# Summing graph messages per node: plain f32 products with the message stationary, and a transposed aggregate

## The chip, the cores and the metric

The kernel runs on one core of a Trainium2 chip. The metric is device time in microseconds, the median of several runs. A core has five engines that run side by side, each with its own queue in program order: TensorE (PE; its weight loads are shown apart as PEld), VectorE (DVE), ScalarE (ACT), GpSimd (POOL) and SyncE (SP, which here only issues DMAs).

## What is computed

One layer of message passing on a graph: 12,500 nodes with 64 features, 800,000 edges with 16 features, a source and a destination node.

```python
N, deg, D, De = 12500, 64, 64, 16
E = N * deg

def reference(x, e_attr, src, dst, w_msg, w_upd):
    N, D = x.shape
    m_in = jnp.concatenate([x[src], x[dst], e_attr], axis=-1)
    msg = _silu(m_in @ w_msg)
    agg = _segment_sum(msg, dst, N)
    return _silu(jnp.concatenate([x, agg], axis=-1) @ w_upd)
```

All is f32. Edges come in no order, so the sum over the edges of a node needs a sort or a scatter.

## The kernel before

**Tables.** The product with `w_msg` is split: `x @ w_msg[0:64]` is computed once per node and kept in HBM as `A_d`, from where it is gathered by source; `x @ w_msg[64:128]` is kept in SBUF as `BW`, in 128 buckets of 98 nodes (`NBK`, `BK`), with the 16 rows for the edge features below each bucket's 98. So a tile of 128 edges of one bucket gets its message from one product: a matrix with a one-hot of the destination within the bucket and the 16 edge features (98 + 16 = 114 columns, `KQ`), times the bucket's 114 x 64 block of `BW`, plus the gathered rows of `A_d`.

**Sorting.** 6250 columns of 128 edges each go through steps of 8 columns (`M`). A step makes one-hots of the bucket (`onehot`, L392 and L393), running sums of them (`sums`, L399 to L406, bf16), ranks by matmuls (`count`, L419 to L422, and `ranks`, L427), spreads the edge records over slots (`expand`, L440) and moves them into bucket order by f32 matmuls (`move`, L460). A finished block is scattered to the store `st` in HBM by an indirect DMA on POOL (`scatter`, L483).

**Batches.** When buckets hold enough edges, a group of 64 tiles is formed on the core (`Group`): a work list says which bucket and which tile, in units of 1, 2 or 4 consecutive tiles (`u`; `QU` = 4 for most of the run: 656 of 818 batches). SP reads the list and loads the records into `rt`. A batch is 8 tiles (6 with units of 2). Its steps lie in four successive periods: `gather` (one indirect DMA of POOL per tile, L643) and `onehot` (L648) in the first; `transpose` of the one-hots (L657, copied by ACT at L660) and `product` (L666) in the second; `message` (DVE adds the gathered rows, L672; ACT takes the silu, L673) and `parts` in the third; `reduce` and `add` in the fourth.

**The sums before.** For units of 4, `parts` splits the f32 message into three bf16 parts by two subtractions on DVE (L681), and `reduce` multiplies the one-hot (stationary, 98 columns, read as bf16) with the three parts at once (moving, 192 columns, L692), summing over the unit's four tiles in PSUM. `add` folds the three parts (L705) and adds each unit's 98 x 64 block to the aggregate `ACC` at an offset read from the list (L707). For units of 1 and 2 the product is plain f32 with the one-hot stationary and the message moving (L694), two passes a product. The last 16 batches, one tile per bucket, add with one instruction (L699).

**Order.** It is written out by hand in `period`: each period issues, for the batches and steps at their several stages, gathers and the scatter on POOL, then the rest, engine by engine in this order. Gather tiles `g` have three buffers (`gp`) and are free again after `message`; PSUM tiles have one buffer each. `next_step` asks for the loads of edge indices (segments of `SEG` columns, in `sg`) and features (`ea`, `rec`, in `eap`) some steps ahead. After the last step come batches alone, and beside the last batches the updates: `Update.run` transposes two buckets of `ACC` at a time (L956), copies them (L958), multiplies with `wu` (L960), adds the stored `x @ w_upd[0:64]` (L962), and takes the silu.

Of the kernel before, what the change touches and what calls it, by code (L numbers as in the profile page):

```python
# [3 lines left out]
F32 = mybir.dt.float32  # L4
# [29 lines left out]
QU = 4  # L34

# [5 lines left out]
SEG = 15 * M  # L41
# [5 lines left out]
def mpnn_kernel(tc, x, e_attr, src, dst, w_msg, w_upd, out):  # L47
# [23 lines left out]
    with es:  # L71
# [17 lines left out]
        io_i = cp.tile([P, P], I32, name="io_i")  # L89
# [7 lines left out]
        ident = cp.tile([P, P], F32, name="ident")  # L97
# [13 lines left out]
        nc.vector.tensor_scalar(out=b64, in0=ipf, scalar1=float(D), scalar2=None, op0=OP.mult)  # L111

# [17 lines left out]
        wu = cp.tile([P, 2, D], F32, name="wu")  # L130
        wx = cp.tile([P, 2, D], F32, name="wx")
# [5 lines left out]
        sent = cp.tile([P, 32, R], F32, name="sent")  # L137
# [26 lines left out]
        class Nodes:  # L164
# [27 lines left out]
            def product(t, ps, w, c):  # L192
                for i in range(0, t.n, 2):
                    nc.tensor.matmul(ps[0:BK, i * c:(i + 2) * c], t.xt[:, i // 2 * BK:(i // 2 + 1) * BK], w.rearrange("p k c -> p (k c)"), start=True, stop=True)  # L194
                return ps[0:BK, 0:t.n * c].rearrange("p (i c) -> p i c", c=c)
# [28 lines left out]
        eap = pool("eap", 3)  # L224
# [92 lines left out]
        for w in (wab, wx, wu):  # L317
            nc.gpsimd.memset(w, 0.0)
# [12 lines left out]
        ACC = lp.tile([BK, NBK, D], F32, name="ACC")  # L331
        ACCf = ACC.rearrange("p b d -> p (b d)")
# [7 lines left out]
        zeros = [RT[i].rearrange("p a c -> p (a c)") for i in range(len(RT))] + [ACC[:, b:b + ZP, :].rearrange("p b d -> p (b d)") for b in range(0, NBK, ZP)]  # L340

        def later():
            z = zeros.pop(0)
            nc.scalar.activation(z, done0[0:z.shape[0], :].to_broadcast(z.shape), AF.Copy)
            if len(zeros) == 7:
                for k in range(P // 32):
                    nc.sync.dma_start(st_t[D0:D0 + DUM, k * 32 * R:(k + 1) * 32 * R], sent[0:DUM].rearrange("p a b -> p (a b)"))
            elif len(zeros) == 5:
                nc.sync.dma_start(BW[BK:KQ], w_msg[2 * D:2 * D + DE, None, :].to_broadcast([DE, NBK, D]))
            elif not zeros:  # L350
                for k in range(2):
                    nc.sync.dma_start(wx[k * D:(k + 1) * D, k, :], w_upd[0:D, :])
                    nc.sync.dma_start(wu[k * D:(k + 1) * D, k, :], w_upd[D:2 * D, :])
# [7 lines left out]
        rbp = pool("rbp", 6)  # L361
        qp = pool("qp", 4)
        qtp = pool("qtp", 2)
        gp = pool("gp", 3)
        mp = pool("mp", 2)
# [124 lines left out]
        class Group:  # L490
# [82 lines left out]
            def middle(g):  # L573
# [5 lines left out]
                elif g.k == 1:  # L579
# [3 lines left out]
                    nc.tensor.matmul(g.ps[0:1, gu:2 * gu], b64, mat[:, 0:gu], start=True, stop=True)  # L583

            def rows(g):
                gu = g.gu
                g.row, g.rb = wp.tile([1, GT], I32, name="row"), rbp.tile([1, GT], I32, name="rb")
# [124 lines left out]
        def period(step=None, batch=None, ptr_new=None):  # L712
# [44 lines left out]
            if a:  # L757
                a.parts()
# [410 lines left out]
```

## Time and profile before

| | |
|---|---|
| median of 3 runs | 11796.37 us (11699.31 to 11822.43) |
| span of the profiled execution, first to last instruction | 9112.0 us |
| POOL busy, and its 6322 gathers | 6777.5 us, 6201.1 us |
| DVE busy, and its 1312 subtractions of L681 | 8127.3 us, 904.8 us |
| PE busy, and its 5248 bf16 passes of L692 | 8088.1 us, 582.4 us |
| ACT busy | 5111.9 us |
| mean granted TensorE clock | 0.963 |

The span is that of the profiled execution; its time around the span is not given apart, and the median of the runs is 2684 us longer than the span. In the profile, a line of a group reads: source line, engine, operation, out<-in with shapes, count, then busy microseconds and mean nanoseconds of one, then the engine's idle time just before them and what ended it. A line of stretches has the stretch and its length, then busy time and instruction count of PE, PEld, DVE, ACT and POOL, the granted clock, the DMA share and GB/s. A line of waits reads: engine, tile and line that waited, what released it, microseconds in total, times, longest. A line of the timeline has start and length in microseconds.

### The profile page before, as it was taken

To read this page: it belongs to the slowest core of one execution; us is meant where nothing else is said; L and a number is where in the kernel's file an instruction comes from. 1 tells how busy PE (TensorE), PEld (TensorE's weight loads), DVE (VectorE), ACT (ScalarE), POOL (GpSimd) and SP (SyncE) were. 2 spreads that over 40 slices of the span, in tenths; PEclk is the share of its full clock that TensorE was granted. 3 is DMA by queue.
4 is the path that set the end of the run, shared out by engine and by line. 5 is a ranking of instruction groups with operands and counts; after the bars stand their busy time and mean duration, and the time that the engine had idled before them with its cause. 6 is when DMAs were issued, how large, how long until landed. Compare 5 with 4: busy or idle time off the path is not lost. (4 is left out here: it accounts for less than half of the span.)

```text
span 9112.0 us, 146201 instructions
## 1 busy us (share of the span) xinstructions
PE 8088.1 (89%) x43940; PEld 5887.5 (65%) x44702; DVE 8127.3 (89%) x17569; ACT 5111.9 (56%) x12617; POOL 6777.5 (74%) x6910
## 2 busy tenths in 40 slices
PE   8999999888988889888888888899888889888677
PEld 5777776666666666666666666666666666666676
DVE  8999999999999999999999999999999999998332
ACT  7666665555555555555555555555555555555222
POOL 1677777777777777777777777777777777777776
PEclk9999999999999999999999999999999999999566
DMA  3222221222221212211222212121212122121223
GB/s 75 55 60 60 62 63 51 52 53 53 53 53 51 56 49 54 56 50 50 54 53 53 55 51 53 52 56 49 55 50 55 51 54 54 51 55 47 58 47 50
DMA packets 650600, 492.45 MB, mean 54 GB/s; under 512 B 482888, under 2 KB 519304, under 8 KB 649800
## 3 DMA queue, kind: packets, MB, share of 16 engines
q0 software_dynamic: 238976, 349.72, 14.6%
q1 hardware_dynamic: 410503, 133.17, 6.7%
q8 instruction: 359, 5.88, 0.3%
q14 instruction: 442, 3.61, 0.1%
q10 hardware_dynamic: 320, 0.07, 0.0%
HBM read 330.05 MB, written 152.30 MB: 53 GB/s over the span
## 5 line engine op out<-in xcount | busy, mean ns | idle before, releaser
L643 POOL DMA_INDIRECT g<-A_d,sidx x6322 | 6201.1, 981 | 1947.5 <-issue 1473.6
L460 PE MATMUL pl<-X,hf 128*128 128x291 f32 (+5 forms) x12512 | 4093.8, 478 | 0.0
L460 PEld LDWEIGHTS pl<-X,hf 128*128 128x128 f32 x12512 | 2307.4, 191 | 1291.7 <-issue 937.8
L440 DVE TENSOR_TENSOR X<-cb,rec 128x442 f32<-128x442 f32 (+5 forms) x3128 | 2647.4, 909 | 27.1
L392 ACT ACTIVATE hf<-iof,shi 128x128 f32<-128x128 f32 x6256 | 1909.2, 389 | 1047.9 <-PE pl L460 1044.5
L666 PEld LDWEIGHTS pre<-w,qt 114*128 114x128 f32 x10496 | 1296.0, 195 | 317.3 <-issue 291.5
L666 PE MATMUL pre<-w,qt 114*128 114x64 f32 x10496 | 1268.9, 275 | 42.2 <-DVE msg L672 42.2
L673 ACT ACTIVATE msg<-msg 128x512 f32<-128x512 f32 (+1 forms) x818 | 501.9, 614 | 1276.8 <-DVE msg L672 1274.2
L672 DVE TENSOR_TENSOR msg<-pre,g 128x512 f32<-128x512 f32 (+1 forms) x818 | 546.1, 668 | 496.5 <-DMA g<-A_d,sidx 298.0
L660 ACT ACTIVATE qt<-tq 114x1024 f32<-114x1024 f32 (+1 forms) x818 | 801.8, 980 | 333.5 <-PE tq L657 330.1
L427 DVE TENSOR_REDUCE rank<-z 128x8 f32<-128x1024 f32 x782 | 949.2, 1214 | 29.9 <-PE z L422 28.1
L420 PE MATMUL z<-G,onesb 128*128 128x384 bf16 x1564 | 516.6, 330 | 486.4 <-DVE G L401 430.7
L681 DVE TENSOR_TENSOR msg<-msg 128x512 f32<-128x512 f32 x1312 | 904.8, 690 | 22.8
L393 ACT ACTIVATE hf<-hf,ones 128x1024 f32<-128x1024 f32 x782 | 899.0, 1150 | 25.4
L465 ACT ACTIVATE blk<-pl 128x512 f32<-128x512 f32 (+1 forms) x568 | 325.4, 573 | 1044.8 <-PE pl L460 911.1
L657 PE MATMUL tq<-ident,q 128*114 128x128 f32 x6322 | 887.9, 286 | 14.3 <-ACT nodes L190 13.0
L657 PEld LDWEIGHTS tq<-ident,q 128*114 128x114 f32 x6322 | 783.5, 142 | 140.8 <-ACT nodes L190 20.4
L692 PE MATMUL ag<-msg,q 128*98 128x192 bf16 x5248 | 582.4, 253 | 298.0 <-DVE rb L589 116.2
L483 POOL DMA_INDIRECT st<-blk,ptrs x567 | 568.7, 1003 | 322.4 <-issue 134.5
L648 DVE TENSOR_TENSOR q<-cb,lo 128x784 f32<-128x784 f32 (+1 forms) x818 | 768.5, 940 | 0.6
L692 PEld LDWEIGHTS <-q 128*98 128x98 bf16 x5248 | 497.7, 126 | 387.7 <-issue 327.9
L420 PEld LDWEIGHTS <-onesb 128*128 128x128 bf16 x1564 | 152.6, 98 | 424.3 <-DVE G L401 318.9
(145 smaller groups left out, 6694.0 us busy)
## 6 DMA issues: line engine op xcount, KB each, us to landing
g<-A_d,sidx POOLq DMA_INDIRECT x6322
ea<-in_e_attr SPq DMA_DIRECT2D x260, 192.0 KB
rt<-st SPq DMA_DIRECT2D x1312, 34.0 KB
st<-blk,ptrs POOLq DMA_INDIRECT x567
rt<-st SPq DMA_DIRECT2D x434, 8.5 KB
nodes<-in_x SPq DMA_DIRECT2D x62, 98.0 KB
rt<-st SPq DMA_DIRECT2D x320, 17.0 KB
A_d<-nodes SPq DMA_DIRECT2D x32, 98.0 KB
```

Source lines behind the costliest of these rows:

```text
L392: nc.scalar.activation(c.hf[:, k, :], iof, AF.Square, bias=c.hi[:, k:k + 1])
L393: nc.scalar.activation(c.hf, c.hf, AF.Relu, bias=ones, scale=-1.0)
L427: nc.vector.tensor_reduce(out=c.rank, in_=c.z, axis=AX.X, op=OP.max)
L440: nc.vector.tensor_tensor(out=c.x[:, k:k + 2, 2:2 + n * R].rearrange("p k (s c) -> p k s c", c=R), in0=hit[:, k:k + 2, 0:n, None].to_broad ...
L460: nc.tensor.matmul(pl[:, 0:w], c.hf[:, k, :], c.x[:, k, 0:w], start=(whole and n == c.size - 1), stop=ends)
L643: nc.gpsimd.indirect_dma_start(out=t.g[:, i, :], out_offset=None, in_=A_d, in_offset=bass.IndirectOffsetOnAxis(ap=t.grp.sidx[:, k:k + 1], ...
L648: nc.vector.tensor_tensor(out=t.q[:, 0:n, 0:BK], in0=ioB[:, None, 0:BK].to_broadcast([P, n, BK]), in1=t.grp.lo[:, i0:i0 + n, None].to_broa ...
L657: nc.tensor.transpose(t.tq[0:KQ, j * P:(j + 1) * P], t.q[:, j, :], ident)
L660: nc.scalar.activation(t.qt[:, 0:w], t.tq[0:KQ, 0:w], AF.Copy)
L666: nc.tensor.matmul(t.pre[:, i * D:(i + 1) * D], t.qt[:, i * P:(i + 1) * P], w, start=True, stop=True)
L681: nc.vector.tensor_tensor(out=t.msg[:, k + 1, :], in0=t.msg[:, k, :], in1=up[:, k, :, 1], op=OP.subtract)
L692: nc.tensor.matmul(t.ag[0:BK, u * w:(u + 1) * w].rearrange("p (k d) -> p k d", d=D), q[:, i, :], m[:, :, i * D:(i + 1) * D], start=(k == 0 ...
```

## The change

- `message` adds and takes the silu in place in the gather tile `g`; the tiles `msg` and `sum` and the step `parts` (L681) go. `gp` has four buffers in place of three.
- `reduce` is one plain f32 product per tile, whatever the unit: the message (128 edges x 64) is stationary, the one-hot (128 x 98) moving. The result is the transposed sum, 64 features on partitions by 98 nodes. Units go in pairs: one to PSUM partitions 0 to 63, the next to 64 to 127, with their tiles alternating.
- `ACC` becomes 128 partitions x 128 buckets x 98: the transposed aggregate, twice, one copy for each PSUM half. `add` adds a unit's 64 x 98 block from PSUM to the copy of its half; the fold L705 goes. The group's list `rb` gets a second row of offsets (steps of 98), made by one more small matmul.
- `Update.run` uses `ACC` as the stationary operand of one product per bucket, with `w_upd[64:128]` stored twice on 128 partitions (which adds the two copies): the transposes and their copy go.
- `ACC` takes more room, so other things shrink: segments of 72 columns, not 120 (`SEG`), two buffers of `ea` and `rec`, not three, five of `rb`, not six, a sentinel block of half the size written in eight DMAs, not four, `ident` and `wx` share room with other tiles, and the loads of `w_upd` come after the last step.

```diff
 QU = 4
+SR = 16
...
-SEG = 15 * M
+SEG = 9 * M
...
-        eap = pool("eap", 3)
+        eap = pool("eap", 2)
...
-        ACC = lp.tile([BK, NBK, D], F32, name="ACC")
-        ACCf = ACC.rearrange("p b d -> p (b d)")
+        ACC = lp.tile([2 * D, NBK, BK], F32, name="ACC")
+        ACCf = ACC.rearrange("p b k -> p (b k)")
...
-                for k in range(P // 32):
-                    nc.sync.dma_start(st_t[D0:D0 + DUM, k * 32 * R:(k + 1) * 32 * R], sent[0:DUM].rearrange("p a b -> p (a b)"))
+                for k in range(P // SR):
+                    nc.sync.dma_start(st_t[D0:D0 + DUM, k * SR * R:(k + 1) * SR * R], sent[0:DUM].rearrange("p a b -> p (a b)"))
...
-        rbp = pool("rbp", 6)
+        rbp = pool("rbp", 5)
...
-        gp = pool("gp", 3)
-        mp = pool("mp", 2)
+        gp = pool("gp", 4)
...
+                    nc.tensor.matmul(g.ps[0:1, 2 * gu:3 * gu], b98, mat[:, 0:gu], start=True, stop=True)
...
             def message(t):
-                w = t.n * D
-                t.msg = mp.tile([P, 3, BT * D], F32, name="msg")
-                u_ = t.msg[:, 2, :]
-                nc.vector.tensor_tensor(out=u_[:, 0:w], in0=t.pre[:, 0:w], in1=t.g.rearrange("p a b -> p (a b)")[:, 0:w], op=OP.add)
-                nc.scalar.activation(t.msg[:, 0, 0:w], u_[:, 0:w], AF.Silu)
-
-            def parts(t):
-
-                t.split = t.grp.u == QU
-                if t.split:
-                    up = t.msg.bitcast(BF16).rearrange("p k (f two) -> p k f two", two=2)
-                    for k in range(2):
-                        nc.vector.tensor_tensor(out=t.msg[:, k + 1, :], in0=t.msg[:, k, :], in1=up[:, k, :, 1], op=OP.subtract)
+                m = t.g[:, 0:t.n, :].rearrange("p a b -> p (a b)")
+                nc.vector.tensor_tensor(out=m, in0=t.pre[:, 0:t.n * D], in1=m, op=OP.add)
+                nc.scalar.activation(m, m, AF.Silu)
+
+            def half(t, j):
+
+                return slice(j % 2 * D, (j % 2 + 1) * D)
 
             def reduce(t):
                 t.ag = pag.tile([P, 512], F32, name="ag")
-                w = 3 * D
...
-                    if t.split:
-                        nc.tensor.matmul(t.ag[0:BK, u * w:(u + 1) * w].rearrange("p (k d) -> p k d", d=D), q[:, i, :], m[:, :, i * D:(i + 1) * D], start=(k == 0), stop=(k == t.grp.u - 1))
-                    else:
-                        nc.tensor.matmul(t.ag[0:BK, u * D:(u + 1) * D], t.q[:, i, 0:BK], t.msg[:, 0, i * D:(i + 1) * D], start=(k == 0), stop=(k == t.grp.u - 1))
+                u = t.grp.u
+                for j in range(0, t.n // u, 2):
+                    for k in range(u):
+                        for v in range(j, min(j + 2, t.n // u)):
+                            i = v * u + k
+                            nc.tensor.matmul(t.ag[t.half(v), v // 2 * BK:(v // 2 + 1) * BK], t.g[:, i, :], t.q[:, i, 0:BK], start=(k == 0), stop=(k == u - 1))
 
             def add(t):
...
-                s = t.ag[0:BK]
-                if t.split:
-                    nu = BT // QU
-                    s = mp.tile([BK, nu * D], F32, name="sum")
-                    nc.vector.tensor_reduce(out=s.rearrange("p (u d) -> p u d", d=D), in_=t.ag[0:BK, 0:nu * 3 * D].rearrange("p (u k d) -> p u d k", k=3, d=D), axis=AX.X, op=OP.add)
-                for u, a in enumerate(t.at(ACCf, ENG.DVE)):
-                    nc.vector.tensor_tensor(out=a, in0=s[:, u * D:(u + 1) * D], in1=a, op=OP.add)
+                for v, r in enumerate(regs(t.grp.rb[:, 1, :], t.i0 // t.grp.u, t.n // t.grp.u, ENG.DVE, (NBK - 1) * BK)):
+                    a = ACCf[t.half(v), ds(r, BK)]
+                    nc.vector.tensor_tensor(out=a, in0=t.ag[t.half(v), v // 2 * BK:(v // 2 + 1) * BK], in1=a, op=OP.add)
...
-            if a:
-                a.parts()
...
+        for k in range(2):
+            nc.sync.dma_start(wx[k * D:(k + 1) * D, k, :], w_upd[0:D, :])
+            nc.sync.dma_start(wu[k * D:(k + 1) * D, :], w_upd[D:2 * D, :])
...
-                for q in range(0, n, 2):
-                    nc.tensor.transpose(z[:, q // 2 * BK:(q // 2 + 1) * BK], ACC[:, b0 + q:b0 + q + 2, :].rearrange("p b d -> p (b d)"), ident[0:BK, 0:BK])
-                at = t.buf[:, BT * D:BT * D + BT // 2 * BK]
-                nc.scalar.activation(at[:, 0:(n + 1) // 2 * BK], z[:, 0:(n + 1) // 2 * BK], AF.Copy)
-                for q in range(0, n, 2):
-                    nc.tensor.matmul(z[0:BK, (BT + q) * D:(BT + q + 2) * D], at[:, q // 2 * BK:(q // 2 + 1) * BK], wu.rearrange("p k d -> p (k d)"), start=True, stop=True)
+                for q in range(n):
+                    nc.tensor.matmul(z[0:BK, q * D:(q + 1) * D], ACC[:, b0 + q, :], wu, start=True, stop=True)
```

64 lines of the change are left out of this document (32 added, 32 removed).

## The prediction

> **What bounds the kernel now.** I read the page first, then the busy time by stretch, then who waits on the gathering engine, then groups and timeline of one stretch. The page's chain of waits covers only the end of the run, where no edge is being sorted any more, so it says nothing of the rest.
>
> ```profile
> span 9112.0 us, 146201 instructions
> PE 8088.1 (89%) x43940; PEld 5887.5 (65%) x44702; DVE 8127.3 (89%) x17569; ACT 5111.9 (56%) x12617; POOL 6777.5 (74%) x6910
> ```
>
> By this line PE and DVE look like the bound and POOL does not. The next rows correct that. They are busy times of three stretches: batches of units of 2 tiles beside the sorting of edges (400 to 1150), units of 4 beside the sorting (1600 to 8350), and batches alone (8450 to 9060). Below them stands what POOL waited for in the middle stretch.
>
> ```profile
> 400.00:1150.00 750.00, 722.20 (x4374) 567.87 (x4458) 709.75 (x1893) 487.40 (x1217) 570.05 (x590) 1.00 0.24 61
> 1600.00:8350.00 6750.00, 6035.73 (x32382) 4254.91 (x32983) 6356.42 (x13123) 3881.29 (x9637) 5158.38 (x5220) 0.99 0.20 53
> 8450.00:9060.00 610.00, 445.12 (x2581) 422.30 (x2579) 212.99 (x560) 149.15 (x295) 457.15 (x481) 0.64 0.28 52
> ...
> POOL g L643 <- issue: 1103.0, 3617, 0.3
> POOL g L643 <- DMA g<-A_d,sidx: 260.4, 854, 0.3
> ```
>
> The longest wait in front of a POOL instruction is 0.3 us and the mean is 1103.0/3617 = 0.305 us: this is no wait for data but the step from one indirect DMA to the next, whatever releaser the view names. Counted in, POOL is full: 5158.38 + 5220 x 0.305 = 6750.5 of 6750 us, and 570.05 + 590 x 0.305 = 750.0 of 750. So the gathers and scatters on POOL set the pace in both stretches, to the microsecond, while PE stands at 96% in the first and 89% in the second, and DVE at 95% and 94%. An edit gains only what it takes off a POOL instruction, and loses only where another engine comes to need more than POOL's period.
>
> Groups of the middle stretch (busy time, mean in ns):
>
> ```profile
> L643 POOL DMA_INDIRECT g<-A_d,sidx x4819 | 4756.8, 987 | 1469.5 <-issue 1103.0 <-DMA g<-A_d,sidx 260.4 <-DVE q L648 44.5
> L483 POOL DMA_INDIRECT st<-blk,ptrs x401 | 401.9, 1002 | 122.3 <-issue 109.5 <-ACT blk L465 6.1 <-ACT rec L268 3.0
> L648 DVE TENSOR_TENSOR q<-cb,lo 128x784 f32<-128x784 f32 x603 | 583.2, 967 | 0.0
> L681 DVE TENSOR_TENSOR msg<-msg 128x512 f32<-128x512 f32 x1206 | 831.6, 690 | 21.0
> L705 DVE TENSOR_REDUCE sum<-ag 98x128 f32<-98x384 f32 x602 | 329.3, 547 | 0.0
> L707 DVE TENSOR_TENSOR ACC<-sum,ACC 98x64 f32 x1204 | 274.9, 228 | 43.7 <-DVE ACC L707 2.1 <-DVE sum L705 0.3 <-issue 0.3
> ```
>
> 603 one-hots are 603 batches, so a period lasts 6750/603 = 11.19 us, and 8 gathers of 0.987 + 0.305 with 0.665 scatters of 1.002 + 0.305 make 11.2.
>
> **What the change takes from POOL.** The gathers are as many as before. But they are not all equally long. POOL and DVE on the timeline from 3021 us on (start, length, engine):
>
> ```profile
> 3021.13 0.94 POOL L643 DMA_INDIRECT g<-A_d,sidx  x1 [0.30 <-issue]
> 3022.38 1.34 POOL L643 DMA_INDIRECT g<-A_d,sidx  x1 [0.30 <-issue]
> 3025.28 0.94 POOL L643 DMA_INDIRECT g<-A_d,sidx  x1 [0.30 <-issue]
> ...
> 3021.49 1.41 DVE L681 TENSOR_TENSOR msg<-msg 128x512 f32<-128x512 f32 x2
> 3022.82 0.97 DVE L648 TENSOR_TENSOR q<-cb,lo 128x784 f32<-128x784 f32 x1
> 3025.47 0.69 DVE L672 TENSOR_TENSOR msg<-pre,g 128x512 f32<-128x512 f32 x1 [0.55 <-DMA g<-A_d,sidx]
> ```
>
> A gather that starts while the two subtractions of L681 run (from 3021.49 for 1.41 us) takes 1.34 us in place of 0.94. One beside L672, also 512 elements wide, takes 0.94. L681 reads two operands from SBUF, L672 one from PSUM and one from SBUF. [...]
>
> The change drops L681 (the two subtractions that split a message in three bf16 parts) for every batch of units of 4. The means of the gather in the two stretches without L681 in their periods, the first with all the sorting on DVE, the second with DVE nearly idle (17 batches of it still have L681), and L681 in the second and in the whole run:
>
> ```profile
> L643 POOL DMA_INDIRECT g<-A_d,sidx x506 | 486.0, 961 | 154.3 <-issue 115.3 <-DMA g<-A_d,sidx 20.1 <-DVE G L401 5.5
> ...
> L643 POOL DMA_INDIRECT g<-A_d,sidx x476 | 453.1, 952 | 145.0 <-issue 131.0 <-DMA g<-A_d,sidx 12.5 <-DVE msg L672 0.6
> L681 DVE TENSOR_TENSOR msg<-msg 128x512 f32<-128x512 f32 x34 | 23.6, 693 | 0.6
> ...
> L681 DVE TENSOR_TENSOR msg<-msg 128x512 f32<-128x512 f32 x1312 | 904.8, 690 | 22.8
> ```
>
> So a gather gains between 0.987 - 0.961 = 0.026 and 0.987 - 0.952 = 0.035 us. L681 runs 1312 times in all, that is in 656 batches; 17 of them lie after the sorting, and 639 x 8 = 5112 gathers are touched: 133 to 179 us. I take the middle, 156 us, because the first row holds more bf16 sums per gather (6 gathers to a period, not 8) and the second none. The scatter gains nothing: 1.002 us here, and it is issued away from L681.
>
> **What it gives PE.** L692 (8 bf16 passes of 192 columns a batch) becomes 8 f32 products with the message (64 columns) stationary and the one-hot (98 columns) moving, two passes each. No row has that shape; its mirror (98 stationary, 64 moving, f32) is L694.
>
> ```profile
> 3009.66 1.03 PE L657 MATMUL tq<-ident,q 128*114 128x128 f32 x8
> 3010.58 0.89 PE L692 MATMUL ag<-msg,q 128*98 128x192 bf16 x8
> 3016.43 0.39 PE L456 MATMUL pl<-done,onesb 1*128 1x512 bf16 x1
> 3016.74 2.00 PE L460 MATMUL pl<-X,hf 128*128 128x223 f32 x8
> 3020.68 0.39 PE L419 MATMUL z<-hf,w 128*128 128x512 bf16 x1
> 3020.90 0.32 PE L420 MATMUL z<-G,onesb 128*128 128x384 bf16 x1
> ...
> 9024.72 1.52 PE L694 MATMUL ag<-msg,q 128*98 128x64 f32 x16
> ...
> L657 PE MATMUL tq<-ident,q 128*114 128x128 f32 x4824 | 642.2, 277 | 0.0
> L692 PE MATMUL ag<-msg,q 128*98 128x192 bf16 x4824 | 526.4, 251 | 278.8 <-DVE msg L681 107.2 <-DVE rb L589 106.6 <-DVE wl L550 61.6
> ```
>
> A burst of n passes lasts n - 1 spacings and the last pass's own 0.25 to 0.28 us. L657: (1.03 - 0.28)/7 = 0.107 us for 128 f32 columns, so 98 cost 0.082 and a load of 64, taken at the same rate, 0.054. L694: (1.52 - 0.25)/15 = 0.085, the longer of load and stream, not their sum of 0.136: the next load hides behind the stream. L692: (0.89 - 0.25)/7 = 0.091. New less old per batch: 16 x 0.085 - 8 x 0.091 = +0.63 us if loads hide as in L694 (taken: it is the same pair of sizes, swapped); 16 x 0.136 - 0.73 = +1.45 if they don't; 8 x 0.085 - 0.73 = -0.05 if the two PSUM halves run side by side.
>
> To this comes a change of the array's shape before and after the sums. L456, with one stationary row, is the nearest: 0.31 us to the next start, against 0.22 for the same 512 columns at L419. That is 0.09 a switch, 0.18 a batch. [...] I take +0.63 + 0.18 = +0.81 us.
>
> What PE has to spare in the middle stretch:
>
> ```profile
> PE z L420 <- DVE G L401: 394.3, 394, 2.5
> PE ag L692 <- DVE msg L681: 107.2, 232, 0.6
> PE ag L692 <- DVE rb L589: 106.6, 75, 2.4
> PE ag L692 <- DVE wl L550: 61.6, 62, 1.2
> ```
>
> 669.7/603 = 1.11 us a period, and before each of these 763 waits some 0.17 us of modelled tail (0.277 - 0.107) count as busy: 763/603 x 0.17 = 0.21, together 1.32. POOL's shorter period takes 8 x 0.026 = 0.21 of it. Left are 1.11 us for 0.81, so PE stays behind POOL, with 0.3 us or 3% idle. The stretch of units of 2 shows that 4% idle is enough. There L694 itself turns round, the sum of load and stream stays, and two switches (0.18) fit into the 4% of its period of 8.9 us (506/6 = 84 batches in 750 us).
>
> **The rest.** DVE loses 1.38 + 0.55 + 0.46 us a period and gets two additions of 98 columns from PSUM, by L707 about 0.23 to 0.27 each: some 1.9 us less, so it needs 6356.42/603 - 1.9 = 8.6 of 11 us. Three of the four waits above end with it. These additions read one operand from PSUM, like L672, so they take L681's place on POOL at nothing. The gather's tile is held until the sums are done, one period longer, and has a fourth buffer: POOL can still run as far ahead as now. Zeroing the wider ACC, halved segments, the smaller read-ahead and the end:
>
> ```profile
> L344 ACT ACTIVATE ACC<-done 98x2048 f32<-98x2048 f32 x4 | 7.7, 1924 | 0.0
> ...
> ACT rec L268 <- DMA ea<-in_e_attr: 10.3, 2, 7.5
> ...
> 9100.93 0.91 PE L956 MATMUL z<-ident,ACC 98*128 98x98 f32 x4 [0.79 <-DVE ACC L699]
> 9102.43 2.02 PE L960 MATMUL z<-wu,xu 128*98 128x128 f32 x8 [0.59 <-ACT xu L958]
> ```
>
> 98/64 of 7.7 us is 4 us more on ACT, before POOL is full. Two late loads in the whole run say that a buffer less is not missed: the queue of SP still issues them three periods ahead, and its eight half-size loads of sentinels, 34 more pairs of segment loads and the moved loads of the update weights meet no waiting reader; if one did, it is 7.5 us. The transpose and its copy leave the end (1.5 us from L956 to L960), 16 passes replace 8 there (about +0.8): -0.7 for each of the last three updates, -2 us.
>
> The sum is 9112 - 156 - 2 = 8954 us. The median of the runs, 11796.37 us, lies 2684 us above the span; nothing in the profile shows that part, and I keep it. 11796 - 158 = 11638, taken as 11640 us.
>
> **The rivals.** PE becomes the bound: the loads into half the array don't hide. Then PE needs 1.45 + 0.18 = 1.63 us more where 1.32 are free, 0.31 over POOL's present pace and 0.52 over the new one; without the tails in the slack it is 0.52 over the present. It is worse than before from +1.32 on, and gives nothing from +1.11 on. 639 x 0.31 to 0.52 = +200 to +330 us, 12000 to 12130; I put 12050. For it: the 3% are thin, and a step with the widest blocks has less. Against it: L694 hides its loads. Chance 0.22.
>
> The collisions only move: POOL falls onto the sums of L401 to L403, or the gather's extra is L648's, which starts under the same 1.34 us. Then the gathers stay near 0.98, 0 to 40 us are won, and the time is 11780. For it: the 1.34 us overlap both. Against it: 0.961 with L648 and the sums in every period. Chance 0.16.
>
> A stall in the loads or buffers, or a gain beyond 179 us by the halves in parallel, has 0.05. The forecast has 0.57; its own range is 11560 to 11710, from 179 + 2 and 133 with the runs' scatter of some 50 us about their median.
>
> **The numbers.** 1% is 118 us, about what a measurement can tell here; faster means under 11678. Of the forecast 0.46 lies there and 0.11 within 1%; of the moved collisions 0.02 and 0.13, with 0.01 slower; of the PE bound 0.01, 0.04 and 0.17; of the rest 0.02, 0.01 and 0.02. Sum: 0.51, 0.29, 0.20. The range goes from 11560 to 11860, over the second rival and the mild end of the first; its dear end is left out.
>
> **What would show it.** Right: the gather's mean near 0.955 us in the long stretch, no 1.34 us beside the message's path, POOL still full with 0.305 between, PE at 95 to 97%, 16 passes of the new sums in about 1.55 us, DVE near 78%. Wrong: waits of POOL above 0.3 us on PE's sums, or new passes 0.13 us apart (PE bound); gathers at 0.98 (collisions moved).

## The result, and the profile after

| | before | after | ratio, 95% interval |
|---|---|---|---|
| timed runs of the comparison, median | 11,809.4 us (4 runs) | 10,957.5 us (4 runs) | 0.9294 [0.9257, 0.9331] |
| span of the page | 9,112.0 us | 10,967.9 us | |

The change made the kernel 7% faster, where 1.3% was forecast. The two pages cannot be set against each other: the page of before shows an execution of 9,112 us, the page of after one of 10,968 us, and yet the change is faster. The plain reason is that this program, whichever of the two kernels, runs at two levels, and all runs timed together on one chip show one of them: on three chips the kernel before took 9,090 to 9,113 us, in all other runs (two chips more, and the timed runs above) 11,644 to 11,979. The page of before came from the quick kind, its timed runs and all of after's from the other; whether that page and those timed runs were of one chip is not on record. Each chip was met in one session only, so it is not shown that the level hangs on the chip and not on the session. Of what follows, each pair of numbers is from one kind.

The first lines of the page of after:

```profile
span 10967.9 us, 159910 instructions
PE 9041.8 (82%) x50244; PEld 6180.6 (56%) x50244; DVE 7181.8 (65%) x15722; ACT 5097.6 (46%) x12601; POOL 6586.9 (60%) x6908
```

Its busy times by stretch, from 1600 to 10200 us (units of 4 beside the sorting; the columns are length, busy time and count for PE, PEld, DVE, ACT and POOL, then granted clock, DMA share and GB/s):

```profile
1600.00:10200.00 8600.00, 7360.82 (x40968) 4910.85 (x40968) 5872.43 (x12354) 4157.95 (x10368) 5399.23 (x5649) 0.92 0.19 45
```

What its POOL waited for from 1600 to 8200 us (total, times, longest):

```profile
POOL g L641 <- issue: 1053.5, 3279, 5.3
POOL g L641 <- remote: 633.1, 284, 2.5
POOL g L641 <- ACT qt L658: 333.7, 121, 4.2
```

The prediction's arithmetic for POOL no longer closes: 5399.23 + 5649 x 0.305 = 7122 of 8600 us, 83%. POOL really waits here (2.2 us a time in the second row of waits), DVE is at 68%, PE at 86%, and no engine is full. The timeline of the same execution shows what they wait for (start, length, engine, line, and in brackets the idle time before):

```profile
5006.25 0.20 PE L581 MATMUL ps<-mat,b 128*1 128x16 f32 x2
5007.39 0.38 PE L419 MATMUL z<-G,onesb 128*128 128x512 bf16 x1
5007.60 1.04 PE L655 MATMUL tq<-ident,q 128*114 128x128 f32 x8
5008.69 0.94 POOL L641 DMA_INDIRECT g<-A_d,sidx  x1 [0.30 <-issue]
5009.94 0.94 POOL L641 DMA_INDIRECT g<-A_d,sidx  x1 [0.30 <-issue]
5012.45 0.17 DVE L586 SCALAR_TENSOR_TENSOR row<-ps,iof 1x16 int32<-1x16 f32 x1 [3.64 <-remote]
5012.64 1.02 ACT L658 ACTIVATE qt<-tq 114x1024 f32<-114x1024 f32 x1 [4.00 <-remote]
5012.64 1.20 DVE L424 TENSOR_REDUCE rank<-z 128x8 f32<-128x1024 f32 x1
5012.82 1.54 PE L682 MATMUL ag<-q,g 128*64 128x98 f32 x15 [4.18 <-remote]
```

tq is recorded as done at 5008.6; its reader, ACT, is free and starts 4 us later, at 5012.64. ps (small products that form the next group) is recorded as done at 5006.45; its reader, DVE, is free from 5008.8 on, starts at 5012.45, and comes to z, done at 5007.8, only after that. PE itself stands until 5012.8, apparently because its sums go into the PSUM buffer that ps holds until DVE has read it. "Remote" is the view's word where it finds no signal to name. On the quick kind the same hand-offs take nothing. I put the mean over some 270 to 550 hand-offs of each sort together (1800 to 7800 us), from the later of the recorded end of TensorE's work and of the reader's own instruction before, to the reader's start (pl holds the moved edge records, which ACT copies out):

| us | sums to DVE | z to DVE | tq to ACT | pl to ACT |
|---|---|---|---|---|
| before, quick kind (before_rep) | 0.00 | 0.00 | 0.01 | 0.03 |
| after, quick kind (after_rep) | 0.07 | 0.00 | 0.01 | 0.02 |
| after, other kind (after_timed) | 1.73 | 1.89 | 3.27 | 0.03 |
| before without L681 (before_noparts), other kind | 2.39 | 1.62 | 1.54 | 0.51 |

So on the other kind of chip the readers of the sums, of z and of tq start 1.5 to 3.3 us late on average in these two kernels (over 0.5 us late in 237 to 396 of some 450 cases in after_timed); the copy of pl does not in the changed kernel. With no engine full I take these hand-offs to set the time there. No run takes the lateness away, so this is inferred and not shown. I call those the late chips, the others the quick ones.

### The profile page after: what moved, and what is told of

The parts are those of the page before. It is cut to its first block, busy times and chain, and to the rows that moved or that the text cites. A ratio compares the mean times of both kernels' runs of the same rounds, so it can differ in the third digit from the quotient of the medians.

```text
span 10967.9 us, 159910 instructions
## 1 busy us (share of the span) xinstructions
PE 9041.8 (82%) x50244; PEld 6180.6 (56%) x50244; DVE 7181.8 (65%) x15722; ACT 5097.6 (46%) x12601; POOL 6586.9 (60%) x6908
## 5 line engine op out<-in xcount | busy, mean ns | idle before, releaser
L641 POOL DMA_INDIRECT g<-A_d,sidx x6322 | 5995.0, 948 | 3825.7 <-issue 1748.0
L457 PE MATMUL pl<-X,hf 128*128 128x291 f32 (+5 forms) x12512 | 4481.4, 504 | 297.3 <-issue 289.5
L457 PEld LDWEIGHTS pl<-X,hf 128*128 128x128 f32 x12512 | 2423.4, 201 | 1920.4 <-issue 1539.4
L693 DVE TENSOR_TENSOR ACC<-ag,ACC 64x98 f32 x1938 | 497.4, 257 | 1937.9 <-remote 1443.9
L682 PE MATMUL ag<-q,g 128*64 128x98 f32 x12644 | 893.7, 283 | 434.4 <-remote 273.9
L655 PE MATMUL tq<-ident,q 128*114 128x128 f32 x6322 | 1048.2, 320 | 68.7 <-ACT nodes L193 40.7
L655 PEld LDWEIGHTS tq<-ident,q 128*114 128x114 f32 x6322 | 928.0, 162 | 237.0 <-issue 101.1
L682 PEld LDWEIGHTS ag<-q,g 128*64 128x64 f32 x12644 | 704.6, 157 | 619.0 <-remote 281.5
L416 PE MATMUL z<-hf,w 128*128 128x512 bf16 x1564 | 650.9, 416 | 5.3 <-ACT hf L390 4.7
L668 DVE TENSOR_TENSOR g<-pre,g 128x512 f32<-128x512 f32 (+1 forms) x818 | 541.2, 662 | 100.3 <-issue 60.7
```

The lines of the kernel that those rows point to most:

```text
L457: nc.tensor.matmul(pl[:, 0:w], c.hf[:, k, :], c.x[:, k, 0:w], start=(whole and n == c.size - 1), stop=ends)
L641: nc.gpsimd.indirect_dma_start(out=t.g[:, i, :], out_offset=None, in_=A_d, in_offset=bass.IndirectOffsetOnAxis(ap=t.grp.sidx[:, k:k + 1], ...
L655: nc.tensor.transpose(t.tq[0:KQ, j * P:(j + 1) * P], t.q[:, j, :], ident)
L682: nc.tensor.matmul(t.ag[t.half(v), v // 2 * BK:(v // 2 + 1) * BK], t.g[:, i, :], t.q[:, i, 0:BK], start=(k == 0), stop=(k == u - 1))
```

## The experiments

**Both kernels again, with a profile each.** No edit.

> The kernel before, unchanged, for a trace of an execution whose span can be set against its time. The trace of before had a span of 9112 us while its runs took 11700 to 11833 us; the trace of the changed kernel has a span of 10968 us with a time of 10970, so only 2 us lie around a span. Theory 1 (two modes: the trace of before was a rare fast execution, the timed ones are slow inside the program): span within 10 us of the time, near 11.8 ms, and TensorE's semaphores come late, by 1 us and more after the recorded ends, as in the changed kernel (0.013 us in the trace of before). Theory 2 (2.7 ms lie outside the program of before alone): span near 9112 us beside a time near 11.8 ms, semaphores at 0.013 us.

> The changed kernel, unchanged. If it too has two modes (theory 1), a repeat may fall near 8950 us, the sum of the prediction, with POOL full (gaps of 0.305 us between its DMAs); if it is slow whenever it runs, 10955 to 10970 us again, with gaps on POOL of over 1 us on TensorE's late semaphores.

A quick chip: 9,102.8 and 8,926.5 us, ratio 0.981 (one run each; a second run of before took 9,098.1). That is 176 us gained, where 158 was worked out. Neither theory of before_rep came out as it was stated: the trace is a quick one beside a quick time. But its span, 9,101.0 us, lies 2 us below its time, so nothing like 2.7 ms stands outside of this program. Busy times by stretch, 1600 to 8200 us, of before_rep:

```profile
1600.00:8200.00 6600.00, 5884.99 (x31685) 4152.25 (x32276) 6219.89 (x12845) 3796.74 (x9430) 5043.63 (x5108) 1.00 0.23 53
```

and the group of its gathers there (count, busy time, mean in ns, idle time):

```profile
L643 POOL DMA_INDIRECT g<-A_d,sidx x4715 | 4651.2, 986 | 1436.9 <-issue 1167.8 <-DMA g<-A_d,sidx 172.8 <-DVE q L648 37.5
```

The same two views of after_rep:

```profile
1600.00:8200.00 6600.00, 6138.24 (x37457) 4272.14 (x38061) 5515.65 (x11438) 3884.47 (x9664) 5004.77 (x5235) 0.99 0.24 54
```

```profile
L641 POOL DMA_INDIRECT g<-A_d,sidx x4833 | 4603.1, 952 | 1472.8 <-issue 1186.3 <-DMA g<-A_d,sidx 172.2 <-PE ag L682 29.3
```

And the new sums on its timeline, right behind the transposes:

```profile
5022.29 1.03 PE L655 MATMUL tq<-ident,q 128*114 128x128 f32 x8
5023.26 0.90 PE L682 MATMUL ag<-q,g 128*64 128x98 f32 x16
```

POOL is full in both: 5043.63 + 5108 x 0.305 and 5004.77 + 5235 x 0.305 are 6601 of 6600 us. The gather went from 986 to 952 ns. 5112 gathers by 0.034 us are 174 us, nearly the whole gain.

**Is it the second operand in SBUF?** The changed kernel with the two subtractions back on DVE as idle work, into a scratch tile; once with both operands in SBUF (after_sub), once with the second in PSUM (after_psum). Room for the scratch comes from a smaller tile of sentinels, written in more pieces.

```diff
# after_sub
+            def parts(t):
+                if t.grp.u == QU:
+                    for k in range(2):
+                        scr = mp.tile([P, BT, D], BF16, name="scr")
+                        nc.vector.tensor_tensor(out=scr, in0=t.g, in1=t.g.bitcast(BF16).rearrange("p a (b two) -> p a b two", two=2)[:, :, :, 1], op=OP.subtract)
...
# after_psum
+                        nc.vector.tensor_tensor(out=scr, in0=t.g, in1=cb.rearrange("p (a b) -> p a b", b=D), op=OP.subtract)
```

They ran first on a late chip, beside the changed kernel, and later on a quick one.

> The changed kernel, unchanged, timed against the kernel before on one chip. Theory C (POOL sets the pace, L681 lengthened its gathers): 8926 against 9098 us, ratio 0.981, in every round. Rival (the 0.929 of the first comparison is the change itself): ratio 0.93 again. If some executions fall into the mode with late TensorE semaphores, both kernels are some 2000 us longer in it.

> The changed kernel with two subtractions of L681's kind put back at their old place, both operands in SBUF, results unused (bf16 scratch; sentinels in 32 smaller DMAs for room). Theory C: the gathers' mean goes from 0.952 back to about 0.985 us in the long stretch and the time rises by 0.033 x 5112 = 170 us, to about 9095. Rival D (it is DVE's load or the order of work that the change relieved, not the operands): a rise too, but the same one with a PSUM operand. Rival E (the gathers' length has nothing to do with it): 8926.

> The same two subtractions, of the same length, with the second operand from PSUM. Theory C: the gathers stay at 0.952 us and the time at 8926 (within 20). Rival D: as long as with two SBUF operands, about 9095.

> after_sub again: the changed kernel with the two subtractions of 8x64 per partition put back as idle work on DVE, both operands in SBUF. Where the changed kernel takes 8,926 us: the gathers go from 952 to about 977 ns as in after_sub, and 5,112 of them by 0.025 us make +128 us, so 9,020 to 9,080; if the subtractions cost nothing there, 8,920 to 8,960. Where it takes about 11,050: 11,050 to 11,150 as before.

> after_psum again: the same two subtractions with the second operand in PSUM. Where the changed kernel takes 8,926 us: DVE is as busy as in after_sub_b, but the gathers stay near 950 ns, so 8,920 to 8,960; if DVE's time and not the operands' place made the cost, the time of after_sub_b. Where it takes about 11,050: 11,050 to 11,180.

| | late chip | quick chip |
|---|---|---|
| before | 11,915.3 | 9,106.3 |
| after | 11,102.1, ratio 0.931 [0.9254, 0.9366] | not run beside them; 8,926.5 for after_rep |
| after_sub | 11,124.6, ratio 0.933 [0.9274, 0.9388] | 9,111.0, ratio 1.0006 [0.9997, 1.0016] |
| after_psum | 11,142.9, ratio 0.935 [0.929, 0.9404] | 8,948.9, ratio 0.983 [0.9813, 0.9846] |

On the quick chip the subtractions with two SBUF operands cost 162 us against those with one operand in PSUM. after_psum takes 22 us more than after_rep did on another chip; 17.6 of these lie before the first gather, which starts at 223.3 us in place of 205.7, with the sentinels written in more pieces. after_sub starts about as late (221.8), which is part of why it lies above its range of 9,020 to 9,080. Without that its subtractions take back some 160 to 170 of the 176 us. The groups of the subtractions and the gathers from 1600 to 8200 us, of after_sub_b:

```profile
L676 DVE TENSOR_TENSOR scr<-g 128x512 bf16<-128x512 f32 x1182 | 815.7, 690 | 20.6
L642 POOL DMA_INDIRECT g<-A_d,sidx x4726 | 4647.3, 983 | 1440.2 <-issue 1151.6 <-DMA g<-A_d,sidx 207.5 <-PE ag L689 29.9
```

A piece of its timeline:

```profile
3004.91 0.94 POOL L642 DMA_INDIRECT g<-A_d,sidx  x1 [0.30 <-DMA g<-A_d,sidx]
3005.27 1.41 DVE L676 TENSOR_TENSOR scr<-g 128x512 bf16<-128x512 f32 x2
3006.16 1.34 POOL L642 DMA_INDIRECT g<-A_d,sidx  x1 [0.30 <-issue]
```

The same groups of after_psum_b:

```profile
L677 DVE TENSOR_TENSOR scr<-g,cb 128x512 bf16<-128x512 f32 x1210 | 826.6, 683 | 20.9
L643 POOL DMA_INDIRECT g<-A_d,sidx x4833 | 4601.9, 952 | 1472.8 <-issue 1171.0 <-DMA g<-A_d,sidx 210.6 <-PE ag L690 31.4
```

And its timeline:

```profile
3006.61 0.94 POOL L643 DMA_INDIRECT g<-A_d,sidx  x1 [0.30 <-DMA g<-A_d,sidx]
3007.25 1.40 DVE L677 TENSOR_TENSOR scr<-g,cb 128x512 bf16<-128x512 f32 x2
3007.86 0.94 POOL L643 DMA_INDIRECT g<-A_d,sidx  x1 [0.30 <-issue]
```

DVE is busy for the same 1.4 us beside the gather in both; what differs is its second operand, and the gather takes 1.34 or 0.94 us. This pair does not part the operand's place from its form: in after_sub, as in L681, it is the upper half of each f32 value of an SBUF tile, read as bf16; in after_psum it is plain f32. Other instructions speak for the place, but say that it does not cost the same each time. In after_rep the 487 gathers that start beside L398, with both operands in SBUF, take 1.02 us on average, the 573 beside L693, with one in PSUM, 0.944. In before_rep the 137 that start beside L707, both operands in SBUF but only 98x64, take 0.95. On the late chip the gathers showed the same thing (975 against 950 ns in that stretch), and it cost next to nothing, since POOL was waiting there anyway.

**The subtractions alone.** The kernel before without L681; the sum takes the first part three times, so one part is counted thrice and two are left out.

```diff
                 if t.split:
-                    up = t.msg.bitcast(BF16).rearrange("p k (f two) -> p k f two", two=2)
-                    for k in range(2):
-                        nc.vector.tensor_tensor(out=t.msg[:, k + 1, :], in0=t.msg[:, k, :], in1=up[:, k, :, 1], op=OP.subtract)
+                    pass
...
-                        nc.tensor.matmul(t.ag[0:BK, u * w:(u + 1) * w].rearrange("p (k d) -> p k d", d=D), q[:, i, :], m[:, :, i * D:(i + 1) * D], start=(k == 0), stop=(k == t.grp.u - 1))
+                        nc.tensor.matmul(t.ag[0:BK, u * w:(u + 1) * w].rearrange("p (k d) -> p k d", d=D), q[:, i, :], m[:, 0:1, i * D:(i + 1) * D].to_broadcast([P, 3, D]), start=(k == 0), stop=(k == t.grp.u - 1))
```

> The kernel before without the two subtractions (L681); the first bf16 part stands three times in the products, so the lower parts of the message are left out. Theory C: all of the gain, about 8930 us, gathers at 0.952, though the sums stay bf16 with the one-hot stationary. Rival F (the gain lies in the new sums, the lighter add or the update): near 9098.

It met a late chip: 12,020.9 against 11,915.3 us, ratio 1.008 [1.0049, 1.0111]. Leaving out L681 gains nothing there. Its waits of POOL, 1600 to 8200 us:

```profile
POOL g L643 <- DVE msg L672: 1530.8, 301, 13.4
POOL g L643 <- issue: 969.5, 3145, 1.8
POOL st L483 <- ACT blk L465: 245.1, 94, 5.1
```

POOL waits for L672 to free a gather buffer, 5 us a time, up to 13.4. This suggested the fourth buffer as the cause of the 7%, which the next experiment tried.

**What gives the 7% on a late chip?** Four kernels on the second late chip: plain f32 sums alone (one line, `t.split = False`); the kernel before with four g buffers; the changed kernel with the two units of a batch one after the other in one PSUM half; and the changed kernel with 16 one-column matmuls more per batch.

```diff
# before_plain
-                t.split = t.grp.u == QU
+                t.split = False
# before_gp4 (and sentinels in 32 pieces, not 4)
-        gp = pool("gp", 3)
+        gp = pool("gp", 4)
# after_onehalf
-                for j in range(0, t.n // u, 2):
+                w = 1 if u == QU else 2
+                for j in range(0, t.n // u, w):
...
+            def at_half(t, v):
+                if t.grp.u == QU:
+                    return slice(0, D), v
+                return t.half(v), v // 2
...
-                        for v in range(j, min(j + 2, t.n // u)):
+                        for v in range(j, min(j + w, t.n // u)):
# after_extra
+                if u == QU:
+                    for i in range(16):
+                        nc.tensor.matmul(t.ag[t.half(i), 500:501], t.g[:, i // 2, :], t.q[:, i // 2, 0:1], start=True, stop=True)
```

> The kernel before with one line changed: batches of units of 4 are summed as those of the units of 1 and 2 are, by one plain f32 matmul per tile (L694), with the one-hot stationary; the two subtractions of L681 and the sum of the three parts (L703 group) go, the place of the aggregate, the three g buffers and the use of one PSUM half stay. On a chip where the kernel before takes about 9,100 us, all theories expect about 8,930 (the subtractions gone, as for the change). On a chip where it takes about 11,900 us: theory A (what the change gains there comes from leaving the three bf16 parts) expects a ratio near 0.93; theory B (it comes from the fourth gather buffer) and theory C (from two units side by side in two PSUM halves) expect 0.99 to 1.01.

> The kernel before with four g buffers in place of three (room for it comes from a smaller tile of sentinels, which is written in more pieces). On a chip where the kernel before takes about 9,100 us: no change by more than 20 us, since POOL never waits for a buffer there. On a chip where it takes about 11,900 us, where POOL waited 2,447 us in all for L672 to free a buffer: theory B expects a ratio near 0.94, theories A and C 0.99 to 1.01.

> The changed kernel, but the two units of a batch of units of 4 are summed one after the other in the same PSUM half, not alternating between two; the same instructions in number and size. On a chip where the changed kernel takes about 8,925 us: 16 passes take about 1.5 us in place of 0.90, of which PE has 0.8 us free per period, so 8,925 to 9,000. Where it takes about 11,100 us: theory C expects about 11,900, theories A and B 11,050 to 11,250.

> The changed kernel with 16 more matmuls of one column (and their 16 weight loads) right after the 16 sums of a batch of units of 4, into PSUM columns nobody reads. If TensorE's late signals come of the number of its instructions in that place (theory D: it works through them at about 7 a microsecond), the run is some 16/7 = 2.3 us longer in each of 656 batches, +1,000 to +1,500 us, where the changed kernel takes about 11,100; if they do not, under +150. Where it takes about 8,925: 32 short instructions in PE's slack of 0.8 us a period, 0 to +150.

| | us | ratio to before (11,735.5) |
|---|---|---|
| before_plain | 11,683.1 | 0.996 [0.9934, 0.999] |
| before_gp4 | 12,390.5 | 1.058 [1.0519, 1.0644] |
| after_onehalf | 10,995.6 | 0.938 [0.9334, 0.9431] |
| after_extra | 12,114.6 (one run) | 1.032 |

So theories A, B and C fall: neither the f32 sums without parts, nor the fourth buffer, nor the two halves gives the 7% by itself. The changed kernel itself was not run on this chip; its ratios elsewhere are 0.929 and 0.931. The halves do shorten the sums: in after_onehalf the same 16 passes, all in one half, take 1.56 us, where those of after_rep and after_timed take 0.90.

```profile
3001.37 1.56 PE L689 MATMUL ag<-q,g 128*64 128x98 f32 x16
```

But this changes the time little. before_gp4 is even 5.8% (655 us) slower than the kernel before. About 100 us of that belong to the sentinels' 32 pieces, which POOL issues near the end within 94 us (12 us for 4 pieces in before_plain) and which delay the first gather by 14 us; the rest goes with the fourth buffer. Its waits of POOL, to be read against those of before_noparts above:

```profile
POOL st L484 <- ACT blk L466: 1737.8, 290, 18.6
POOL g L644 <- issue: 990.0, 3246, 0.5
POOL g L644 <- DMA g<-A_d,sidx: 64.6, 212, 0.3
```

The wait for a buffer is all but gone in this stretch, and POOL now stands at the scatter, for a block that ACT copies out of TensorE's result: 1738 us, 6 us a time. The wait only changed its place; why the whole became longer is not known. In after_extra the time came where theory D put it (+1,119 us over after_onehalf, 1.7 us a batch), but not by its reason (no run shows its 7 a microsecond): the sums' signals came almost at once there (0.04 us), and TensorE stood between its own instructions, for nothing that the trace shows. From 2000 to 8000 us of that run, waits of PE:

```profile
PE ag L685 <- issue: 546.1, 750, 1.3
PE ag L682 <- remote: 95.5, 25, 4.3
```

TensorE hardly waits for another engine there: its busy time (5221.65 us) and these 546 us make 96% of the 6000. So with more to do it seems to have become the bound itself, and the run says little about why signals are late.

**The rest of the change, apart.** before_inplace is the kernel before with plain f32 sums, the message made in place in g and four buffers, but the operands not turned; after_gp3 the changed kernel with three g buffers; the two kernels called lateadd move the adds to the aggregate behind `e.place` in DVE's order.

```diff
# before_inplace (beside gp 4 and t.split = False)
-                t.msg = mp.tile([P, 3, BT * D], F32, name="msg")
...
+                m = t.g[:, 0:t.n, :].rearrange("p a b -> p (a b)")
+                nc.vector.tensor_tensor(out=m, in0=t.pre[:, 0:t.n * D], in1=m, op=OP.add)
+                nc.scalar.activation(m, m, AF.Silu)
# after_lateadd, before_lateadd
-            if r:
-                r.add()
             if z:
                 z.expand()
...
                 e.place(ptr_new)
+            if r:
+                r.add()
```

> The kernel before with plain f32 sums (as in before_plain) and with the message made in place in g, four g buffers and no message buffer, as in the changed kernel; the one-hot stays stationary and the aggregate stays as it was. What is left between this and the changed kernel is the place of the operands (message stationary, one-hot moving, aggregate transposed). Where the kernel before takes about 11,800 us: if the place of the operands gives the 7%, the ratio is 0.99 to 1.01 as for before_plain; if the message in place gives it, 0.93 to 0.95. Where the kernel before takes about 9,100: POOL sets the pace and 8,930 is expected, as for the change.

> The changed kernel with the two adds of the sums to the aggregate (L693) moved behind the move of the bucket counts and the placing in DVE's order, so that DVE does not stand still for the late signal of the sums before it makes G. Theory E (where TensorE's signals come late, the pace is a loop: sums, late signal, L693, L434, L437, L398, z, tq, sums; the period follows its length) expects, where the changed kernel takes about 11,050, 1 to 2 us off a period of 12.3 us, so 9,700 to 10,600. If the loop is not what sets the pace: 10,950 to 11,150. Where the changed kernel takes about 8,925: within 30 us of it.

> The kernel before with the sum and the adds (L703 group, L707) moved in the same way in DVE's order; nothing else of the change. Theory E expects, where the kernel before takes about 11,800 us, a gain of the sum's 0.55 and the adds' 0.48 us and of the late signal ahead of them, 2 to 3 us of a period of 13.5: 9,800 to 10,700. If not: 11,700 to 11,900. Where it takes about 9,100: within 30 us.

> The changed kernel with three g buffers in place of four. g is held until the sums now, so a batch's gathers wait for the sums two periods back. Where the changed kernel takes about 8,925 us: L682 of the batch three before ends about 9.1 us after its message starts, with 1.9 us left before the gathers begin, so 8,925 to 9,050. Where it takes about 11,050 and the buffers matter: 11,600 to 12,200; if they do not, 11,000 to 11,150.

> before_inplace again, for a chip on which the kernel before takes about 11,800 us: ratio 0.99 to 1.01 if the turned operands give the 7% there, 0.93 to 0.95 if the message in place in g does. Where the kernel before takes about 9,100: 0.98 as before.

> after_lateadd again, for a chip on which the changed kernel takes about 11,050 us: theory E (a loop through DVE's wait for the late signal of the sums sets the pace) expects 9,700 to 10,600, no loop there 10,950 to 11,200. Where the kernel before takes about 9,100: 9,070 as before.

All of these met quick chips, both times.

| | first | second |
|---|---|---|
| before | 9,101.9 | 9,106.3 |
| before_inplace | 8,936.2, ratio 0.982 [0.9798, 0.9831] | 8,941.1, 0.982 [0.9804, 0.9837] |
| after_gp3 | 8,940.2, 0.982 [0.9801, 0.984] | |
| after_lateadd | 9,067.7, 0.996 [0.9949, 0.9977] | 9,066.4, 0.996 [0.9942, 0.9975] |
| before_lateadd | 9,300.1, 1.022 [1.0196, 1.0236] | |

On a quick chip the gain needs neither turned operands nor halves: before_inplace, which has plain f32 sums, the message in place and four buffers, has all but 10 us of it (8,936.2 against 8,926.5, on two chips). Plain sums alone (before_plain) met no quick chip. Busy times of before_inplace from 1600 to 8200 us:

```profile
1600.00:8200.00 6600.00, 6339.47 (x37255) 4665.96 (x37857) 5332.10 (x11340) 3878.98 (x9653) 5007.12 (x5228) 1.00 0.23 54
```

Its transposes and sums on the timeline:

```profile
2999.46 1.04 PE L657 MATMUL tq<-ident,q 128*114 128x128 f32 x8
3000.34 1.52 PE L692 MATMUL ag<-g,q 128*98 128x64 f32 x16
```

PE needs 96% of the time here, and POOL is still full (5007.12 + 5228 x 0.305 = 6602): the sums at 1.52 us instead of 0.90 cost nothing. The turned operands and the halves save TensorE 0.6 us a batch that no one waits for, on this kind.

The lateadd kernels were expected within 30 us of the kernels that they vary on a quick chip. They lose 141 us to the changed kernel and 198 to the one before, most of it before 1600 us: 276 to 289 instructions of POOL per 400 us from 400 to 1600 us, in place of 311 to 317. Waits of PE, and the longest of POOL for another engine, in after_lateadd, 400 to 1100 us:

```profile
PE ps L575 <- DVE ACC L693: 52.7, 18, 3.9
PE ps L579 <- DVE ACC L693: 23.8, 17, 1.7
...
POOL g L641 <- PE ps L575: 89.0, 18, 7.6
```

The sums and the small products that form the next group share one PSUM buffer (`ag`). An add that comes later holds the buffer longer, the forming of groups, on which the gathers' indices hang, comes late, and POOL waits for it. Whether the move gains on a late chip was not seen.

## Why the prediction was wrong, point by point

- **The step that failed: "the median of the runs, 11796.37 us, lies 2684 us above the span; nothing in the profile shows that part, and I keep it".** These 2684 us are not outside of the program. Around a span lie some 2 us (the run of 10,970.1 us has a span of 10,967.9; on the late chip of after_timed the kernel before took 11,836.8 with a span of 11,835.0). The timed runs were executions in which the program itself takes 11.8 ms, and the page showed another. Of the kernel before no trace of the late kind was kept; in those of its variants and of the changed kernel the readers of TensorE's results start late, and POOL, which the prediction took to set the pace, is 83% full in the changed kernel. The change acts differently there: it took 852 us off, not 158, a ratio of 0.93 and not 0.98. A gap of 29% between a page and its runs should have been taken as a sign that another bound may hold in the runs, and should have had a rival of its own; none of the rivals, a stall or a larger gain at 0.05 included, was of that kind.
- **POOL sets the pace, and the gathers beside L681 are slow: right, and in size too, for the execution that the page shows.** 9112 - 158 = 8954 was forecast for it; 8,926 to 8,949 came on three quick chips, for the changed kernel and three kernels without subtractions of two SBUF operands (after_gp3, after_psum, before_inplace). The gather's mean was forecast at 955 and is 952 ns, and nothing between the gathers is above 0.315 us. The gain per gather was taken as the middle of 0.026 and 0.035 us; it was 0.034, near the second: with the subtractions gone the other sorting adds little to the mean (952 ns in the long stretch, 944 from 8300 to 8870 us with no sorting). The row that I took as the dear end, 961 in the units of 2, is 955 there now.
- **That it is the second operand of the subtractions: shown**, by after_sub_b against after_psum_b on one chip (9,111.0 and 8,948.9 us). That it is the operand's place in SBUF alone, and not also its bf16 form, is likely but not parted by this pair. Of the instructions with both operands in SBUF, the gather takes 1.34 us in place of 0.94 beside L681 and 1.02 on average beside L398; beside the short L707 it shows no cost (0.95).
- **The cost on PE: one term mis-sized, without effect on a quick chip.** +0.63 us a batch was taken for the passes and 0.18 for two switches. The 16 passes last 0.90 us where the 8 old ones lasted 0.89, so the first term is nearly nothing: the end of the bounds with the halves side by side (-0.05) was nearly the true one, and the serial price is what the passes take in one half (1.56 us in after_onehalf). The switches are there, in their forecast size. From the start of the last transpose to that of the first sum it is 0.203 us in after_rep (median) and 0.109 in before_inplace, where the sums' stationary operand has 98 columns, not 64; from the last sum to the move behind it, 0.176 and 0.087. That is 0.09 each, 0.18 a batch, and PE's busy time per batch rose by 6138.24/604 - 5884.99/590 = 0.19 us. PE is at 93% instead of 95 to 97, and the rival of a PE bound was not met; even at 96%, in before_inplace, PE stays behind POOL.
- **DVE near 78%: it is at 84%** (5515.65 of 6600). I added up the rows' lengths (1.9 us less), but DVE's instructions overlap on the trace (in that of before, L681 ends at 3022.90 us and L648 starts at 3022.82): the busy time per batch fell by 6219.89/590 - 5515.65/604 = 1.41 us (590 and 604 one-hots).
- **The fourth buffer at nothing: right on a quick chip.** Three give 8,940 us, four 8,926 on another chip.
- **The collisions only move: not met.** Of 4,833 gathers of the long stretch none takes over 1.2 us; before_rep had 360 of 4,714.
- **What gives the 7% on a late chip is not settled.** It is not the subtractions (ratio 0.933 with them in after_sub, 1.008 without them in before_noparts), not plain f32 sums alone (0.996), not the fourth buffer alone (1.058, some 0.01 of it by the pieces), not the halves (0.938 without alternation). What is left is the message in place, the turned operands, or parts of the change that help only together; the two runs meant to part them met quick chips. One observation points to the stretch: on late chips the changed kernel is no faster in units of 2 (384 POOL instructions in the 700 us from 400 on, against 389) and 12% faster in units of 4 (3955 against 3535 in the 6000 us from 2000 on). Both stretches are counted in after and before_noparts, on two late chips.
- **Why TensorE's signals come late on some chips is open too.** The mean granted clock is lower on the late chips (0.89 in after_timed, 0.96 in after_rep), but a lowered clock does not bring the lateness in the trace: in after_timed ACT starts on tq 3.6 us late on average where the clock had been full for the 8 us before (371 cases), 2.4 us where it had been halved for 3.5 us of them or more (56 cases). One trace of another kind goes with the lateness: on the quick chip nearly every signal of DVE is in the record (7,388 of 7,450 in after_rep, 1600 to 8000 us), on a late one less than half (2,892 of 6,167 in after_timed). Whether the missing records and the late starts have one cause, no run shows.

## What to carry to other kernels

Before you work out a gain from a page, compare its span with the timed runs: here a span lies 2 us below the time of its own run. If the difference is far larger, the page may show another bound than the runs have, and every chance should be split over both. When POOL's indirect DMAs set the pace, look at what DVE reads beside them: beside two subtractions with two SBUF operands a gather took 1.34 us here (after_sub_b), beside two of the same size with one operand in PSUM 0.94 (after_psum_b). When a wait is taken away and the time does not fall, look where the engine stands next: a fourth buffer moved POOL's wait to the scatter (1738 us in before_gp4). And before you move an instruction later, look at what it keeps occupied: a later add held a shared PSUM buffer, on which TensorE (52.7 and 23.8 us) and then POOL (89.0 us) came to wait from 400 to 1100 us of after_lateadd.

## What was not expected of the hardware

- The same program runs at two levels: 9,090 to 9,113 us on three chips, 11,644 to 11,979 us on two. In the kernels of the table above the readers of TensorE's results (z, tq, sums) start 0.0 to 0.1 us after its recorded ends on the first kind, and 1.5 to 3.3 us after on the second, on average.
- With two units summed in two PSUM halves, 16 f32 passes of 98 columns take 0.90 us (after_rep), against 1.56 us for the same passes in one half (after_onehalf). Around sums with a stationary operand of 64 columns 0.09 us more goes by on each side (0.203 and 0.176 us in after_rep) than around those with 98 (0.109 and 0.087 in before_inplace).
- A buffer more, with its sentinels in more pieces, made a kernel slower by 5.8% on a late chip (before_gp4).
